# Three homes instead of two for a pair of experts' row indices, weights and flags

## The chip, the cores and the metric

The kernel runs on one core of a Trainium2 chip. The metric is the device time of one execution in microseconds (us); a kernel is represented by the median of its runs.

## The reference

Three layers follow each other: attention with a position bias, a dense MoE layer with the activation h·sigmoid(h), and a second MoE layer in which each token is routed to two of eight experts. The change lies in the last one:

```python
def _moe2_ref(x, w_gate, w_noise, noise, w1, w2):
    logits = x @ w_gate
    noise_scale = np.log1p(np.exp(x @ w_noise))
    noisy_logits = logits + noise_scale * noise
    top2 = np.argpartition(-noisy_logits, 2, axis=1)[:, :2]
    ...                                    # top2_w: softmax over the two
    for e in range(E):                     # E = 8, D = 512, F = 1024, 1152 tokens
        for k in range(2):
            mask = top2[:, k] == e
            h = np.maximum(x[mask] @ w1[e], 0.0)
            out[mask] += top2_w[mask, k, None] * (h @ w2[e])
```

## The kernel before, in words

Attention and the dense layer fill roughly the first 500 us. The last 240 us or so are the second MoE layer, and only they matter here.

The eight experts are taken as four pairs, g = 0 to 3; "pair 3" is experts 6 and 7. Each expert has 320 slots for its tokens. The loop at L1044 traces, for each pair g below 3, three things side by side: `experts(g)` (the products of this pair), `conv_pair(g + 1)` (the weights of the next pair) and `gather_pair(g + 1)` (the token rows of the next pair). A scheduler then fixes one order of instructions per engine, from its own model of times; at run time every engine and every queue goes through its list in that order, and an instruction that waits holds up all that stand behind it on the same engine.

For one pair the steps are:

- `gather_pair`: DVE makes 0/1 tables of slots (`one_hot`, L816); PE turns them into sums (`place`, L827, tile `pm`); DVE turns the sums into row numbers. That is `locate`: L840 writes `idx`, L842 `far` (a flag for an empty slot), L843 the second half of `idx`, and L849 and L850 write `ws`, the routing weights.
- `fetch`: POOL issues five gathers of token rows (L859, `gx<-yrows,idx`, 128 rows of 1024 fp16 values), and SP issues for each a transposing DMA into `xg` (L861). There are four `gx` buffers, so the fifth gather needs the first transpose done. A transpose waits for its gather.
- `conv_pair`: for each of the pair's four matrices, four loads of 512 KB on the SP queue (L909 for a first matrix, L911 for a second, tile `stg`, four buffers); ACT writes the high fp16 half (L923), DVE the low half (L924), which frees the `stg` buffer.
- `experts`: `up` is 16 blocks of 12 matmuls (L979 to L981) into one of three PSUM buffers `ph`. ACT writes the high half of the hidden rows (L985) and DVE the low half (L986); a `ph` buffer is free when both have read it. `down` (L995 to L997) and `down_last` (L1010) multiply by the second matrices into `po`; ACT scales a finished `po` by `ws` into `ot` (L964), and POOL adds it to the rows of `out` by an indirect DMA that reads the row numbers from `idx` (L958, "scatter" below). A pair has six scatters, and each waits for the one before it to land.

The homes of `idx`, `ws` and `far` for pair 0 are fixed (L884, L885, they show as `room`). Pairs 1, 2 and 3 call `slots_for`, which takes them from a pool with a number of buffers under one tag. With two buffers, pair 3 gets the ones that pair 1 had, so `locate` of pair 3 (L840) can write only when all that reads pair 1's is over; the last of that is pair 1's sixth scatter.

Of the kernel before, what the change touches and what calls it, by code (L numbers as in the profile page):

```python
# [9 lines left out]
F32 = mybir.dt.float32  # L10
F16 = mybir.dt.float16
I32 = mybir.dt.int32
# [4 lines left out]
DRAM = bass.MemoryType.DRAM  # L17
# [13 lines left out]
TOFF = 569  # L31
# artanh(s) / s = 1 + sum ARTANH[k] (4 s^2)^(k + 1) on 0 <= s <= 1/3, to float32
ARTANH = [0.0833333445274358, 0.012499649295167536, 0.0022356941233917663, 0.0004185089430942374, 0.00011865690887866284]
# [47 lines left out]
def shape_constants():  # L81
    """Tables that follow from the shapes alone."""
    f = np.float32
    pos = np.arange(S)
    lrel = np.log1p(pos.astype(f)).astype(f)
    psi = np.log1p(np.maximum(pos.astype(f), f(1.0))).astype(f)
    u = np.arange(TW)
    dist = np.abs(u[None, :] - TOFF - 2 * np.arange(4)[:, None])
    key = np.concatenate([256 * m + 2 * np.arange(n) + t for m, n in ((0, 128), (1, 128), (2, 32)) for t in range(2)])
    p = np.arange(128)  # L90
    row = np.zeros((128, NTT), f)
    for c in range(4):
        for b in range(B):
            row[:, 2 * c + b] = b * S + I0[c] + p
    row[:64, 8] = 512 + p[:64]
    row[64:, 8] = S + 512 + p[:64]
    return {
        "imax": np.ascontiguousarray(np.maximum(pos, 1).astype(f)[None, :] - f(0.5)),
        "ldist": np.log1p(dist.astype(f)).astype(f),
        "xij": (lrel[np.abs(pos[:, None] - key[None, :])] / psi[:, None]).astype(f),  # L100
        "bd": np.ascontiguousarray(np.repeat(np.eye(4, dtype=f), HID, axis=0)),
        "tri": (p[:, None] < p[None, :]).astype(np.float16),
        "eye": np.eye(128, dtype=np.float16),
        "iota": np.broadcast_to(np.arange(1, CAP + 1, dtype=np.float16), (128, CAP)).copy(),
        "row": np.ascontiguousarray(np.stack([1 + np.arange(NTT)[None, :] * 128 + p[:, None], row + 1], -1).astype(f)),
    }


def body(ctx, tc, nc, A):
    out = A["out"]  # L110
# [3 lines left out]
    def STT(eng, o, x, scale, y, op=OP.subtract):  # L114
        """o = x * scale - y"""
        if eng is G and scale == 1.0:
            G.tensor_tensor(o, x, y, op=op)  # L117
        else:
            V.scalar_tensor_tensor(o, x, scale, y, op0=OP.mult, op1=op)

    def after(later, earlier):
        """later issues behind earlier on their engine"""
        tc.add_manual_dep(later.ins, earlier.ins.name, mybir.DependencyInfo(
            mybir.DependencyClass.NoSync, mybir.DependencyReason.DATA), reason="order")
# [24 lines left out]

# [1 line left out]
    def load(name, shape, src, dt=F32, pool=main, eng=SP):  # L151
# [21 lines left out]
    def turn(dst, src, pe, ev):  # L173
        """dst[:, k] = the transpose of src's columns 128k .. 128k + 127."""
        if not pe:
# [10 lines left out]

    # the exponential's table is loaded while the data comes
    warm = at.tile([128, 1], F32, name="warm")
    G.memset(warm, 0.0)
    SC.activation(warm, warm, AF.Exp)  # L190
    # unit c at distance d is on where s*(max(i, 1) - 0.5) > s*tau, with s the sign of b1 and tau integral
    th4 = at.tile([128, 4], F32, name="th4")
# [29 lines left out]

# [1 line left out]
    KM = [at.tile([128, 2, H, 2, 128], F16, name=f"km{b}") for b in range(B)]  # L224
# [57 lines left out]
    def q_prep(c, g):  # L282
        """The first pass' columns of a head hold its high parts twice; the second's the low parts of both batches (or twice)."""
        nb = 2 if c < 4 else 1
# [24 lines left out]

# [1 line left out]
    EB = {c: dram.tile([H, NR[c], S], F32, name=f"eb{c}") for c in range(NCH) if c != ORDER[0]}  # L311

    BR = {}
    # eight places of 8 KB: the first chunk's position bias takes three, then weights in turn
    WB = main.tile([128, 8 * 4096], F16, name="wb")
# [62 lines left out]

# [1 line left out]
    def scores(c, h, qt, qs, pqs):  # L380
        """q k for the batches qs, or for both within a tile."""
        for _ in qs:
# [99 lines left out]

# [1 line left out]
    WT = {}  # L484

    def conv(key, half, src):
        """src(piece) -> DRAM view [128, 512] int64; 8 pieces of 512 columns."""
        hi, lo = wtile(), wtile()
# [35 lines left out]

# [1 line left out]
    wgn = m1.tile([128, 4, 16], F32, name="wgn", tag="th", bufs=NTH)  # L526
# [14 lines left out]
    def moe1(c):  # L541
        """h = x w_in, g = h sigmoid(h), f block by f block."""
        xT = xTs[c]
# [22 lines left out]
    def moe1b(c):  # L566
        """y = g w_out."""
        nb = 2 if c < 4 else 1
# [53 lines left out]
    def run(*gens):  # L622
        """gens: (generator, weight): round robin in proportion to the weights until all end."""
        live = [[g, w, 0.0] for g, w in gens if g is not None]
# [43 lines left out]
    a, b, c, d, e = ORDER  # L668
    # what is traced when: position of the first step, and distance of the steps
    live = {}  # L670

    def merge(until, **more):
        """steps of all that has been given, by position; each waits for the ends of those it names."""
        for name, (gen_, names) in more.items():
# [18 lines left out]
    for x in range(3):  # L693
        i = SP.dma_start(out[384 * x:384 * x + 384].rearrange("(t p) d -> p t d", p=128), zero[:, None, :].to_broadcast([128, 3, DM]))
        follow(i, ZK)
    # small tiles in what the position bias held
    homes = [("mk", 1024)] * 3 + [("btmp", 512)] * 3
# [28 lines left out]

# [1 line left out]
    T3 = [128, NTT, E]  # L728
# [13 lines left out]
    def route(t0, t1, part):  # L742
        """slot: 1 + the token's place among its expert's tokens, 0 for other experts; aux: 1 + its rows in Y and out, and its weight."""
        n = t1 - t0
        ts, T = slice(t0, t1), [128, n, E]
        lg, lx = LG[:, ts, :8], LG[:, ts, 8:]
        # log(1 + exp(x)) = max(x, 0) + 2 artanh(v / (2 + v)), v = exp(-|x|)
        V.scalar_tensor_tensor(u[:, ts], lx, -1.0, lx, op0=OP.mult, op1=OP.max)
# [30 lines left out]
        if part == 0:  # L779
            # later tokens take no slot below 128  # L780
            V.tensor_scalar(carry[:, 1], cnt, 128.0, None, op0=OP.max)
        else:
            V.tensor_tensor(carry[:, 0], carry[:, 1], cnt, op=OP.add)
# [18 lines left out]

# [1 line left out]
    # columns of 128 slots: 0 and 1 the first 128 of either expert, 2 and 3 the next 128, 4 both last 64, 5 the second's last 64 again  # L804
    XG, IDX, OHT, ROW = {}, {}, {}, {}
# [14 lines left out]
    def place(g, parts, f0, f1, pm):  # L820
        """sums over the tokens of aux's columns f0 .. f1, for each slot."""
        pm = pm[:, :6 * (f1 - f0)].rearrange("p (c f) -> p c f", c=6)
# [8 lines left out]
    def locate(g, *parts):  # L831
        """the rows of the slots of these columns, and unless that is urgent their weights; an empty slot reads row 0, and adds to a row past the end."""
        idx, ws = IDX[g]
# [18 lines left out]
    def fetch(g, part):  # L852
        """rows of Y for these slots, transposed."""
        idx = IDX[g][0]
# [8 lines left out]
    def slots_for(g):  # L863
        IDX[g] = (m2a.tile([128, 2, 6], I32, name="idx", tag="idx", bufs=2), m2a.tile([128, 5], F32, name="ws", tag="ws", bufs=2))
        ROW[g] = m2a.tile([128, 6], F32, name="far", tag="far", bufs=2)

    def dense(c):
        """the first MoE layer of one chunk, with the routing of the chunks before it."""
        for f, _ in enumerate(moe1(c)):
# [21 lines left out]

# [1 line left out]
    EW = {}  # L893

    def conv_half(e, half):
        """half 0: the expert's first matrix, 1: its second."""
        p = 4 * (e // 2) + 2 * half + e % 2
# [69 lines left out]
    def experts(g):  # L967
# [3 lines left out]
        def up(k, c0, n):  # L971
            """hidden rows for n columns of xg from c0; the second expert's begin at 320."""
            a_h, a_l = EW[2 * g + k, 0]
# [76 lines left out]
    s_m2.close()  # L1050
# [1 line left out]
    nround = nc.values_load(rounds[0:1, 1:2], min_val=0, max_val=13)  # L1052
# [81 lines left out]
```

## Time and profile before

| | us |
|---|---|
| median of 3 runs | 763.01 |
| the runs | 759.04, 763.01, 767.55 |
| span of the profiled execution (first to last instruction) | 761.8 |
| PE busy in it | 605.9 (80%) |
| DVE, ACT, POOL busy | 501.5, 378.1, 373.2 |
| granted TensorE clock, mean over the span | 0.894 of full speed |

The time of the profiled execution itself is not listed beside its span; the median lies 1.2 us above the span and the three runs lie 8.5 us apart. Times in the views count from the first instruction. A row of a timeline gives start, duration, engine, line, operation, tiles (written <- read), shapes, how many were merged, and in brackets the idle time of the engine before it and what ended it. "SPq" is the queue of DMAs that SP issues; the duration there is that of issuing, not of the transfer. Consecutive matmuls overlap in the records, so their pace is read from start to start.

### The profile page before, as it was taken

The numbers are of one execution on the slowest core, as the hardware profiler recorded it, in microseconds if no ns is written. First come the engines' busy times: TensorE is split into PE (matmuls) and PEld (weight loads), VectorE is DVE, ScalarE is ACT, GpSimd is POOL, SyncE is SP. The second block draws the span as 40 slices with busy tenths as digits, with TensorE's granted clock in tenths as the row PEclk, the third lists the DMA queues.
The fourth block names the chain that finished last, engine by engine and source line by source line (L and its number), as shares of the span: only waits on it lengthen the run. The fifth ranks groups of instructions, "written<-read, shape, count | busy, mean of one in ns | idle before, by whom it ended". The sixth has DMA issues, their size and how long they took to land. (4 is left out here: it accounts for less than half of the span.)

```text
span 761.8 us, 16564 instructions
## 1 busy us (share of the span) xinstructions
PE 605.9 (80%) x6371; PEld 401.7 (53%) x6371; DVE 501.5 (66%) x1093; ACT 378.1 (50%) x805; POOL 373.2 (49%) x366
## 2 busy tenths in 40 slices
PE   0564756568578888988998889969899899699992
PEld 0552434446344666556755665756665555355640
DVE  3999999999999689457943866546766625440200
ACT  2755558777544567355723654751464526241210
POOL 2786677678867687446842541305205122403022
PEclk9775557689698999998999999989999999899996
DMA  6457778779875699886996859635989847743123
GB/s 133 114 153 239 159 165 188 190 198 180 175 187 133 182 181 183 157 165 125 159 222 149 159 114 315 178 129 118 290 261 260 266 128 220 189 111 40 19 25 43
DMA packets 203143, 125.77 MB, mean 165 GB/s; under 512 B 153076, under 2 KB 175732, under 8 KB 203060
## 3 DMA queue, kind: packets, MB, share of 16 engines
q1 hardware_dynamic: 170868, 90.39, 51.2%
q10 hardware_dynamic: 27648, 24.32, 11.2%
q0 software_dynamic: 4544, 9.97, 7.0%
q8 instruction: 51, 0.84, 0.5%
q14 instruction: 32, 0.26, 0.1%
HBM read 74.83 MB, written 18.22 MB: 122 GB/s over the span
## 5 line engine op out<-in xcount | busy, mean ns | idle before, releaser
L117 POOL TENSOR_TENSOR pr<-z,pr 128x512 f16<-128x512 f32 x72 | 94.6, 1319 | 23.3 <-ACT pr L438 14.6
L553 PE MATMUL ph<-xT,wb 128*128 128x256 f16 (+1 forms) x320 | 84.3, 273 | 11.4 <-DVE th L558 5.9
L345 PE MATMUL pb<-rhs_h,mk 128*128 128x64 f16 (+1 forms) x720 | 66.4, 210 | 26.1 <-ACT ta L361 12.1
L337 DVE TENSOR_TENSOR mk<-io,tau 128x1024 f16<-128x1024 f16 (+1 forms) x90 | 85.2, 953 | 0.7 <-PE pb L346 0.7
L117 POOL TENSOR_TENSOR gt<-th,gt 128x256 f16<-128x256 f32 (+1 forms) x80 | 56.5, 709 | 59.3 <-ACT gt L562 56.7
L554 PE MATMUL ph<-xT,wb 128*128 128x256 f16 (+1 forms) x320 | 84.3, 273 | 0.0
L958 POOL DMA_INDIRECT out<-ot,idx x18 | 28.2, 1567 | 114.4 <-ACT ot L964 66.3
L117 POOL TENSOR_TENSOR g<-ta 128x256 f32<-128x256 f32 (+1 forms) x72 | 63.2, 877 | 42.9 <-ACT ta L361 36.0
L555 PE MATMUL ph<-xT,wb 128*128 128x256 f16 (+1 forms) x320 | 84.2, 273 | 0.0
L388 PE MATMUL pq<-km,qt 128*128 128x512 f16 (+2 forms) x160 | 51.5, 436 | 29.3 <-DVE st L431 28.8
L986 DVE SCALAR_TENSOR_TENSOR ht<-ph,ht 128x320 f16<-128x320 f32 (+2 forms) x80 | 32.7, 418 | 62.8 <-ACT ht L985 62.7
L436 ACT ACTIVATE z<-z,st 128x576 f32<-128x576 f32 x72 | 55.3, 768 | 37.2 <-DVE st L435 36.9
L345 PEld LDWEIGHTS <-mk 128*128 128x128 f16 (+1 forms) x720 | 57.9, 112 | 19.5 <-DVE mk L337 7.9
L346 PEld LDWEIGHTS <-mk 128*128 128x128 f16 (+1 forms) x720 | 57.0, 112 | 19.5 <-issue 18.8
L346 PE MATMUL pb<-rhs_l,mk 128*128 128x64 f16 (+1 forms) x720 | 66.0, 210 | 0.0
L924 DVE SCALAR_TENSOR_TENSOR wb<-stg,wb 128x1024 f16<-128x1024 f32 (+1 forms) x48 | 48.1, 1040 | 18.6 <-ACT wb L923 18.5
L985 ACT ACTIVATE ht<-ph 128x320 f16<-128x320 f32 (+2 forms) x80 | 29.5, 379 | 61.2 <-PE ph L981 60.0
L923 ACT ACTIVATE wb<-stg 128x1024 f16<-128x1024 f32 (+1 forms) x48 | 41.9, 908 | 33.5 <-DMA stg<-in_e 33.3
L577 PE MATMUL py<-wb,gt 128*128 128x512 f16 x144 | 56.1, 390 | 1.6 <-POOL wb L511 1.6
L576 PE MATMUL py<-wb,gt 128*128 128x512 f16 x144 | 56.0, 391 | 1.5 <-DVE st L431 1.3
L578 PE MATMUL py<-wb,gt 128*128 128x512 f16 x144 | 55.9, 388 | 0.0
L511 POOL TENSOR_TENSOR wb<-tt,wb 128x512 f16<-128x512 f32 x32 | 43.7, 1366 | 17.2 <-ACT wb L510 17.0
(198 smaller groups left out, 1800.8 us busy)
## 6 DMA issues: line engine op xcount, KB each, us to landing
stg<-in_e SPq DMA_DIRECT2D x64, 512.0 KB, 5.2
raw<-in_w_in ACTq DMA_DIRECT2D x16, 512.0 KB, 4.9
raw<-in_w_out ACTq DMA_DIRECT2D x16, 512.0 KB, 3.7
bt<-eb SPq DMA_DIRECT2D x24, 288.0 KB, 3.4
eb<-g SPq DMA_DIRECT2D x12, 512.0 KB, 3.5
yrows<-yh SPq DMA_DIRECT2D x9, 256.0 KB, 4.2
out<-zero SPq DMA_DIRECT2D x3, 768.0 KB, 5.8
bt<-eb SPq DMA_DIRECT2D x16, 144.0 KB, 2.9
```

The costliest lines, as they stand in the source:

```text
L117: G.tensor_tensor(o, x, y, op=op)
L337: i = V.tensor_tensor(mk[:, :, :n], io16[:, None, i0:i0 + n].to_broadcast([128, 8, n]), tv, op=OP.is_gt)
L345: mm(pb[:n, :, t, :], m, rhs_h, start=True, stop=False)
L346: mm(pb[:n, :, t, :], m, rhs_l, start=False, stop=True)
L388: i = mm(pq[p0:p0 + n, :512].rearrange("p (m s) -> p m s", m=2), lt, KM[b][r0:r0 + nr, :, h].rearrange("p m x s -> p m (x s)"), start=star ...
L436: SC.activation(z, z, AF.Exp, bias=st[:, 2:3], scale=0.125, accum_out=sums[:, bi, h % 4:h % 4 + 1])
L553: mm(ph, hh[:, cs], xh, start=(j == 3), stop=False)
L554: mm(ph, hh[:, cs], xl, start=False, stop=False)
L555: mm(ph, hl[:, cs], xh, start=False, stop=(j == 0))
L576: mm(pys[i], gh, oh[:, cs], start=(f == 0), stop=False)
L577: mm(pys[i], gh, ol[:, cs], start=False, stop=False)
L578: mm(pys[i], gl, oh[:, cs], start=False, stop=(f == 15))
```

## The change

The pool gets three buffers instead of two for the three tiles, so that pairs 1, 2 and 3 each have their own:

```diff
     def slots_for(g):
-        IDX[g] = (m2a.tile([128, 2, 6], I32, name="idx", tag="idx", bufs=2), m2a.tile([128, 5], F32, name="ws", tag="ws", bufs=2))
-        ROW[g] = m2a.tile([128, 6], F32, name="far", tag="far", bufs=2)
+        IDX[g] = (m2a.tile([128, 2, 6], I32, name="idx", tag="idx", bufs=3), m2a.tile([128, 5], F32, name="ws", tag="ws", bufs=3))
+        ROW[g] = m2a.tile([128, 6], F32, name="far", tag="far", bufs=3)
```

All else in the diff are comments and docstrings, which were taken out. Since the scheduler sees fewer dependencies, the order of the instructions changes too, on DVE, POOL and SP, all of it around `locate` and `fetch` of pair 3. (On PE one matmul of a `down` moves behind a block of `up`; on ACT the order stays.)

On DVE, at `locate` of pair 3, as a difference. `ew_9475` is the first matrix of expert 6, `ew_9661` that of expert 7, and L986 writes the hidden rows of pair 2:

```order
-L986 SCALAR_TENSOR_TENSOR ht<-ph,ht 128x320 x3
-L924 SCALAR_TENSOR_TENSOR ew_9475<-stg,ew_9474 128x1024 x4
-L924 SCALAR_TENSOR_TENSOR ew_9661<-stg,ew_9660 128x1024
...
+L986 SCALAR_TENSOR_TENSOR ht<-ph,ht 128x320 x2
 L840 TENSOR_SCALAR idx<-pm 128x5
 L842 TENSOR_SCALAR far<-pm 128x5
...
+L924 SCALAR_TENSOR_TENSOR ew_9475<-stg,ew_9474 128x1024 x4
+L924 SCALAR_TENSOR_TENSOR ew_9661<-stg,ew_9660 128x1024
```

`locate` moved ahead of the low halves of both first matrices of pair 3, eight instructions of L924, and ahead of four of L986. Before, L840 stood behind them and waited for the scatters of pair 1; now the only thing that it waits for is `pm` from PE.

On POOL, at the scatters of pair 1 (`idx_8318` is pair 1's, `idx_9500` pair 3's, `idx_8895` pair 2's), as a difference:

```order
 L958 DMA out<-ot_9307,idx_8318 1152x512
+L859 DMA gx_9763<-yrows_139,idx_9500 128x1024
+L859 DMA gx_9766<-yrows_139,idx_9500 128x1024
+L859 DMA gx_10056<-yrows_139,idx_9500 128x1024
+L859 DMA gx_10059<-yrows_139,idx_9500 128x1024
 L958 DMA out<-ot_9312,idx_8318 1152x512
+L859 DMA gx_10062<-yrows_139,idx_9500 128x1024
 L958 DMA out<-ot_9342,idx_8318 1152x512
```

The five gathers of pair 3 stood behind all six scatters of pair 1; now four stand behind the first scatter and the fifth behind the second.

On SP, the loads of pair 3's weights and the transposes of its rows, as a difference (the eight L909 are the loads of the first matrices of experts 6 and 7, four each):

```order
-L909 DMA stg<-in_e 128x1024 x8
-L911 DMA stg<-in_e 128x2x512 x5
-L861 DMA_TRANSPOSE xg<-gx 128x8x128 x2
-L911 DMA stg<-in_e 128x2x512 x3
-L861 DMA_TRANSPOSE xg<-gx 128x8x128 x3
+L909 DMA stg<-in_e 128x1024 x4
+L861 DMA_TRANSPOSE xg<-gx 128x8x128 x5
+L909 DMA stg<-in_e 128x1024 x4
+L911 DMA stg<-in_e 128x2x512 x8
```

All five transposes now stand between the loads for expert 6 and those for expert 7; before, thirteen loads stood ahead of the first of them.

## Rows read from the trace of the kernel before

**Rows 1.** The page, its first line.

```profile
span 761.8 us, 16564 instructions
```

**Rows 2.** The chain that ended last, 700 us on: start, us, what.

```profile
711.53 16.71 issue
```

**Rows 3.** Stretches: length, busy per engine (x instructions), PE clock, DMA share, GB/s.

```profile
530.00:553.00 23.00, 19.84 (x195) 14.29 (x192) 16.33 (x41) 7.84 (x14) 7.78 (x6) 1.00 1.03 283
618.00:632.00 14.00, 14.00 (x73) 6.92 (x71) 0.99 (x2) 2.71 (x4) 4.65 (x4) 1.00 0.26 31
640.00:653.70 13.70, 7.38 (x47) 4.55 (x47) 6.39 (x16) 8.92 (x13) 3.18 (x2) 0.91 0.79 222
653.70:658.00 4.30, 4.28 (x16) 2.19 (x16) 4.30 (x7) 0.44 (x1) 4.00 (x2) 0.51 0.61 169
658.00:728.00 70.00, 70.00 (x462) 40.05 (x461) 17.21 (x29) 18.21 (x34) 12.63 (x10) 1.00 0.37 75
```

**Rows 4.** Timeline of PE, 638 to 662 us.

```profile
639.95 0.38 PE L995 MATMUL po<-wb,ht 128*128 128x512 f16 x1 [0.32 <-ACT ot L964]
...
647.00 0.38 PE L996 MATMUL po<-wb,ht 128*128 128x512 f16 x1
653.72 0.42 PE L979 MATMUL ph<-xg,wb 128*128 128x320 f16 x1 [6.34 <-DVE ht L986]
...
661.72 0.62 PE L1010 MATMUL po<-wb,ht 128*64 128x512 f16 x4
```

**Rows 5.** Timeline of DVE, 640 to 660 us.

```profile
644.28 1.21 DVE L924 SCALAR_TENSOR_TENSOR ew<-stg,ew 128x1024 f16<-128x1024 f32 x1
652.51 0.17 DVE L840 TENSOR_SCALAR idx<-pm 128x5 int32<-128x5 f32 x1 [7.01 <-issue]
...
653.19 0.47 DVE L986 SCALAR_TENSOR_TENSOR ht<-ph,ht 128x320 f16<-128x320 f32 x1
```

**Rows 6.** Timeline of POOL, pair 1's first and last scatter, pair 3's gathers.

```profile
616.74 1.42 POOL L958 DMA_INDIRECT out<-ot,idx  x1 [18.96 <-ACT ot L964]
...
644.50 2.42 POOL L958 DMA_INDIRECT out<-ot,idx  x1 [6.94 <-ACT ht L985]
652.95 1.01 POOL L859 DMA_INDIRECT gx<-yrows,idx  x1 [6.02 <-DVE idx L843]
654.26 4.13 POOL L859 DMA_INDIRECT gx<-yrows,idx  x1 [0.30 <-issue]
658.70 1.19 POOL L859 DMA_INDIRECT gx<-yrows,idx  x1 [0.31 <-issue]
```

**Rows 7.** Timeline of PE, the sums for pair 3's `locate`.

```profile
615.63 1.59 PE L827 MATMUL pm<-room,oht 128*128 128x5 f16 x51
```

**Rows 8.** Timeline of the SP queue: loads for expert 7, last transpose of pair 3.

```profile
632.75 1.46 SPq L909 DMA_DIRECT2D stg<-in_e  x2
...
671.15 1.25 SPq L861 DMA_TRANSPOSE xg<-gx  x1
```

**Rows 9.** Waits of the SP queue, 612.6 to 640 us: total, times, longest.

```profile
SPq L909 <- DVE ew L924: 22.4, 4, 20.2
```

**Rows 10.** Timelines of POOL and SP, pair 1's first gather and last transpose.

```profile
530.84 1.00 POOL L859 DMA_INDIRECT gx<-yrows,idx  x1 [0.95 <-DVE far L842]
...
551.60 1.25 SPq L861 DMA_TRANSPOSE xg<-gx  x1
```

**Rows 11.** Timeline of ACT, 636 to 660 us: conversions of pair 3's weights.

```profile
638.27 1.06 ACT L923 ACTIVATE ew<-stg 128x1024 f16<-128x1024 f32 x1 [3.39 <-DMA stg<-in_e]
...
651.06 1.06 ACT L923 ACTIVATE wb<-stg 128x1024 f16<-128x1024 f32 x1 [0.23 <-DMA stg<-in_e]
657.11 0.44 ACT L985 ACTIVATE ht<-ph 128x320 f16<-128x320 f32 x1 [5.00 <-PE ph L981]
```

**Rows 12.** Line 909, 632 to 637 us: from issue to landing.

```profile
DMA to landing us min/median/max: 5.5/5.8/6.0
```

**Rows 13.** Line 909, 577 to 584 us, beside pair 2's gathers and transposes.

```profile
DMA to landing us min/median/max: 4.6/6.7/6.9
```

**Rows 14.** Line 861, transposes of pair 0 from 522 to 530 us.

```profile
DMA to landing us min/median/max: 3.1/3.1/3.1
```

**Rows 15.** Line 859, pair 3's gathers, 652 to 662 us.

```profile
DMA to landing us min/median/max: 3.3/4.2/6.9
```

## The prediction, made before the changed kernel was run

> **What bounds the kernel now.** I read the chain that ended last first. The end is a string of scatters, and ahead of it stands one wait of 16.71 us until 728.2 [rows 2], which is POOL waiting for PE's products of pair 3. So the end of the kernel moves with PE. Second, the table of stretches: from 618 to 632 PE is busy all 14.00 us, from 658 to 728 all 70.00 us, but from 640 to 653.7 only 7.38 of 13.70 [rows 3]. Third, PE's timeline shows that this is a single hole: the matmul at 647.00 ends at 647.38, the next starts at 653.72, 6.34 us later, released by L986 on DVE [rows 4]. Fourth, DVE: L924 from 644.28 ends at 645.49, then DVE stands still for 7.01 us until L840 of pair 3 starts at 652.51; the L986 that PE needs stands behind it and runs at 653.19 [rows 5]. The view names no instruction as releaser. What fits is pair 1's sixth scatter, issued at 644.50 [rows 6]: it reads the `idx` that L840 overwrites, and a landing at about 652.4 would be 7.9 us after issue. This is the wait that the change removes. After the hole PE also runs slowly: from 653.7 to 658 the granted clock is 0.51, that is 1.2 of 2.4 GHz, and full again from 658 on [rows 3].
>
> **The change, part by part.**
>
> *The hole.* L840 no longer waits for a scatter and stands before the four-plus-four L924 of pair 3's first matrices. Its only input is `pm`, whose 51 matmuls end at 617.22 [rows 7]; DVE has 0.99 us of work from 618 to 632 [rows 3], so `locate` (about 1 us) lies in idle time and costs nothing; if that cover were gone it would cost its 1 us. At 645.5 DVE goes straight on to L986, and PE's next block finds its `ph` buffer free by about 646. PE keeps its 6.34 us.
>
> *The clock.* The 4.30 us at clock 0.51 follow the hole; ahead of it PE was at full clock (from 640 to 653.7 the mean is 0.91, the fall lies inside the hole) [rows 3]. Without the hole the same work takes 4.30 x 0.51 = 2.2 us, a gain of 2.1. Sum so far 6.34 + 2.1 = 8.4 us.
>
> *Is something else late next on PE?* From 653.72 to the first L1010 at 661.72 PE needs 8.00 us [rows 4], 5.9 at full clock, so L1010 now comes at 647.2 + 5.9 = 653.1. It needs the high half of a hidden block that ACT writes behind its last conversion: that one starts at 651.06, just after its load landed, ends at 652.12, and with 0.44 for L985 the block is ready at 652.6 [rows 11]. So PE does not wait, but has only 0.5 us to spare.
>
> *Gathers, in POOL's queue.* The first follows scatter 1 (616.74 + 1.42) [rows 6] at about 618.5. Four gathers at about 1.3 us each push scatter 2 to 623.7, and the fifth gather follows at about 626.7, when the first transpose has landed. The later scatters of pair 1 move back by some 3 us, and the sixth may start at 648 instead of 644.5. Now only pair 2's first scatter waits for it, and that needs the `down_last` of pair 2, whose first matmuls run at 661.72 [rows 4].
>
> *Transposes, in SP's queue.* This is the price of the change. The four loads for expert 7 went out from 632.75 [rows 8], after the SP queue had stood idle for 20.2 us waiting for DVE to free their buffers [rows 9]. They now stand behind all five transposes. What arrives late hits PE at once: ACT's conversion at 638.27 had already waited 3.39 us for the first of these loads [rows 11], and PE at 639.95 had waited 0.32 us for the L964 behind it [rows 4]. So every us by which these loads land later is a us of PE. Two bounds. Upper: from the first gather to the end of the last transpose pair 3 took 652.95 to 672.40 = 19.4 us [rows 6, 8]. From 618.5 that ends at 637.9, 5.2 us after 632.75, and the load then lands 0.9 us slower (medians 6.7 beside gathers and transposes, 5.8 as it was) [rows 12, 13]: 6.1 us. Lower: gathers land 4.2 us after issue (median) [rows 15], so the first transpose goes out at 622.7 and lands at 626; the fifth gather lands at 630.9, its transpose takes 1.25 to issue and is through at 632.2, half a us before the loads could go anyway: 0. I take 0.5 us, near the lower end, because the stretch resembles that one: DMA share 0.26 from 618 to 632, against 0.61 to 0.79 and 1.03 where the long paces were measured [rows 3], and transposes in a quiet stretch landed after 3.1 us [rows 14]. A gain from this move is excluded: the loads still wait for DVE.
>
> Two rules of the Trainium skill bear on these 0.5 us. The rows first: a load took 0.9 us longer beside gathers and transposes. The page "DMA: Bandwidth & Descriptors", section "Issuing engines are not separate DMA queues", says that DMAs issued by SP and POOL run on the same 16 engines and interleave, which speaks against the change; by it a load that meets the last transpose would cost up to those 0.9 us even if SP issues it in time, and the trace agrees with it. Second, the gather at 654.26 took 4.13 us to issue, beside DVE's L924, and the one after it 1.19 [rows 6]. [...]
>
> **Sum.** 6.34 + 2.1 - 0.5 = 7.9 us. The span of 761.8 [rows 1] becomes 753.9; the median of the runs lies 1.2 above that span, so I predict **755.1 us**, 1.0% less than 763.01.
>
> **The rivals.**
>
> *The loads come late (in part given back).* Between 1 and 6.1 us late by the reckoning above. For it: both measured paces are near 20 us, and the queue is strictly in order. Against: both were measured with weight loads between the transposes and a DMA share above 0.6, where the new place has 0.26. Time: 763.0 - 8.4 + 1 to 763.0 - 8.4 + 6.1, so **755.6 to 760.7**.
>
> *ACT is the next to be late.* The spare 0.5 us at L1010 goes if the loads of expert 6's second matrix, for which ACT waited up to the end (0.23 at 651.06 [rows 11]), land later than before; the delayed scatters 5 and 6 now overlap them. A load 0.9 us slower would cost 0.4, one at 6.9 instead of 5.5 costs 0.9: **755.5 to 756**, too small to be told from the forecast.
>
> *Slower than before.* One mechanism: the fifth gather waits for the first transpose, the fifth transpose for that gather, and behind it on SP stand the loads. In pair 1 the way from the first gather to the end of the last transpose took 530.84 to 552.85 = 22.0 us, at a DMA share of 1.03 [rows 3, 10]. From 618.5 that is 640.5, the loads are 7.7 late and land 0.9 slower, PE stands for 8.6 us from 640 on, falls to half clock as it did after 6.34 us, and pays the 2.1 again: 10.7 lost for 8.4 won, **765.3**. It decides from 6.3 us of lateness on, where lateness and clock together eat the 8.4. For it speaks only that stretch, and it carried nine times the DMA traffic (283 against 31 GB/s, to which the moved gathers and transposes add).
>
> *The change does nothing.* This would need another reader of the old home, or another wait of L840. The order shows three separate homes and `pm` as the only wait: **763**.
>
> **How the numbers follow.** Forecast 0.65, loads late 0.20, ACT late 0.08, slower 0.05, nothing 0.02. The runs of before spread over 8.5 us, so a median of three may be off by some 2.5 us; 1% (7.6 us) is about what can be told from no change. The range runs from 755.1 less 2.5 and a little for a lateness of 0, to the top of the late loads: **752 to 761**. Faster by over 1% means under 755.4: a bit over half of the forecast's 0.65, a third of ACT's 0.08 and little of the others, 0.41. Slower by over 1% means over 770.6, which even the slower rival reaches only with the spread or a longer pace: 0.04. The rest, 0.55, is within 1%, most of it a real gain of some us.
>
> **What would show it.** Right: on DVE L840 of pair 3 starts near 617.5 with no idle time of 7 us before it; PE's hole of 6.34 us is gone, the clock is 1.00 from 640 to 658, and the first L1010 behind it comes at about 653; on SP the fifth transpose is through by 633; ACT's wait for the load that was 3.39 us stays under 4.5. Wrong: the loads for expert 7 go out after 634, or PE stands at 640 for more than 1 us, or a new hole opens between 640 and 665. If the hole is gone and PE gains nothing by 728, the premise that the end moves with PE is wrong.

## The result and the profile after

The changed kernel takes **758.37 us** (median of 17 runs, 749.10 to 766.24), beside 764.80 us for the kernel before timed beside it (17 runs, 759.04 to 770.23). The ratio is **0.9889, 95% interval 0.9863 to 0.9915**; it leaves out four runs of the changed kernel that count as slow, more than 1.5% above its fastest (760.48 to 766.24 us), and the medians of all 17 runs each give 0.9916. The forecast was 755.1 of 763.01, a ratio of 0.9896; the absolute time lies 3.3 us above it and inside the range, partly because the kernel before was itself 1.8 us higher when both were timed together.

The page of the changed kernel opens with:

```profile
span 756.6 us, 16562 instructions
```

That is 5.2 us less than [rows 1], but this execution entered the second MoE layer late: pair 1's first scatter starts at 620.14, against 616.74 in [rows 6], although nothing was changed ahead of it (over the twelve profiled executions of this document it starts between 613.85 and 622.00). So times of after are compared less 3.4 us, and the stage is measured from that scatter to pair 3's first: 616.74 to 728.47 before, 620.14 to 723.38 after, 111.7 and **103.2 us, 8.5 less**. Behind pair 3's first scatter both executions need 33.3 and 33.2 us. Pair 3's first scatter on POOL's timeline, in the kernel before:

```profile
728.47 1.42 POOL L958 DMA_INDIRECT out<-ot,idx  x1 [20.28 <-ACT ot L964]
```

And in the changed kernel:

```profile
723.38 1.43 POOL L958 DMA_INDIRECT out<-ot,idx  x1 [20.26 <-ACT ot L964]
```

Stretches of the changed kernel, with the columns of [rows 3]:

```profile
618.00:632.00 14.00, 14.00 (x120) 7.91 (x119) 1.84 (x9) 3.56 (x6) 7.77 (x7) 1.00 0.78 188
640.00:653.70 13.70, 13.33 (x90) 8.59 (x89) 9.47 (x12) 9.48 (x14) 2.54 (x2) 1.00 1.02 323
653.70:658.00 4.30, 4.30 (x27) 2.09 (x25) 3.05 (x5) 1.71 (x3) 1.57 (x1) 1.00 1.02 360
658.00:723.00 65.00, 65.00 (x433) 37.52 (x431) 15.56 (x27) 17.87 (x33) 9.11 (x6) 1.00 0.20 33
```

PE is busy 13.33 of the 13.70 us in which it had been busy 7.38, and the clock is 1.00 throughout. On DVE's timeline L840 stands early, and L986 follows the fourth conversion of expert 7 without a pause:

```profile
621.51 0.17 DVE L840 TENSOR_SCALAR idx<-pm 128x5 int32<-128x5 f32 x1 [1.74 <-PE pm L827]
...
647.74 1.22 DVE L924 SCALAR_TENSOR_TENSOR ew<-stg,ew 128x1024 f16<-128x1024 f32 x1
648.87 1.12 DVE L986 SCALAR_TENSOR_TENSOR ht<-ph,ht 128x320 f16<-128x320 f32 x2
```

L840 now waits for its sums alone (compare [rows 5]). PE's only gap over 0.25 us between 605 and 700 us is the one that was there before [rows 4], and the first L1010 of pair 2 comes at 653.2 on the old time axis:

```profile
643.41 0.38 PE L995 MATMUL po<-wb,ht 128*128 128x512 f16 x1 [0.37 <-ACT ot L964]
...
656.62 0.62 PE L1010 MATMUL po<-wb,ht 128*64 128x512 f16 x4
```

POOL's timeline: the first scatter of pair 1, the first two gathers of pair 3, and the fifth:

```profile
620.14 1.42 POOL L958 DMA_INDIRECT out<-ot,idx  x1 [19.34 <-DMA stg<-in_e]
621.95 1.02 POOL L859 DMA_INDIRECT gx<-yrows,idx  x1 [0.38 <-DVE idx L843]
623.26 0.98 POOL L859 DMA_INDIRECT gx<-yrows,idx  x1 [0.30 <-issue]
...
630.05 0.98 POOL L859 DMA_INDIRECT gx<-yrows,idx  x1 [1.51 <-DMA xg<-gx]
```

The SP queue: five transposes, then the four loads for expert 7, which stood in front of them before [rows 8]:

```profile
625.32 11.62 SPq L861 DMA_TRANSPOSE xg<-gx  x5
637.03 2.85 SPq L909 DMA_DIRECT2D stg<-in_e  x4
```

The loads go out 16.9 us after pair 1's first scatter, 0.9 later than before (632.75 - 616.74 = 16.0). ACT's conversion nonetheless waits hardly longer, 3.44 us against the 3.39 of [rows 11]:

```profile
641.72 1.06 ACT L923 ACTIVATE ew<-stg 128x1024 f16<-128x1024 f32 x1 [3.44 <-DMA stg<-in_e]
```

And the chain that ended last now runs through the landing of that load, 4.58 us after its issue (in the kernel before the view follows the chain back only to 701 us, so the two can't be compared here):

```profile
637.03 4.58 DMA stg<-in_e
```

### The profile page after: what moved, and what is told of

It reads as the page before. It is cut to its first block, busy times and chain, and to the rows that moved or that the text cites. A ratio compares the mean times of both kernels' runs of the same rounds, so it can differ in the third digit from the quotient of the medians.

```text
span 756.6 us, 16562 instructions
## 1 busy us (share of the span) xinstructions
PE 606.9 (80%) x6371; PEld 402.6 (53%) x6371; DVE 502.3 (66%) x1093; ACT 377.9 (50%) x805; POOL 366.5 (48%) x366
## 4 chain that ended last, share of the span: by engine, by line
PE 29%; DVE 29%; DMA 18%; issue 11%; ACT 4%; POOL 4%; SPq 3%; ACTq 1%; another core or an unknown queue 1%; DVEq 0%; POOLq 0%
DMA stg<-in_e 6%; DVE mk L337 4%; PE ph L979 3%; DVE z L431 3%; DMA pt<-pr 3%; PE ph L981 3%; DVE pr L442 3%; PE ph L980 3%; DVE tt L504 3%; DVE tt L505 3%; PE po L1010 3%; DVE tt L500 2%; PE po L996 2%; PE po L995 2%; PE po L997 2%
## 5 line engine op out<-in xcount | busy, mean ns | idle before, releaser
L553 PE MATMUL ph<-xT,wb 128*128 128x256 f16 (+1 forms) x320 | 84.9, 275 | 11.5 <-DVE th L558 7.1
L986 DVE SCALAR_TENSOR_TENSOR ht<-ph,ht 128x320 f16<-128x320 f32 (+2 forms) x80 | 32.8, 420 | 54.3 <-ACT ht L985 53.8
L924 DVE SCALAR_TENSOR_TENSOR wb<-stg,wb 128x1024 f16<-128x1024 f32 (+1 forms) x48 | 48.3, 1042 | 23.6 <-ACT wb L923 20.2
```

The source lines that it names most:

```text
L553: mm(ph, hh[:, cs], xh, start=(j == 3), stop=False)
```

## The experiments

**The theory.** The third home of `idx` takes away L840's wait for pair 1's last scatter; that wait cost PE a hole and half clock behind it. The price is paid on SP: what pushes back the loads for expert 7 is lost on PE. **Rivals:** another of the three homes counts; the loads have slack; the rows must be early for the gain.

All edits are made to the changed kernel. The table has one profiled execution each: when the first load for expert 7 is issued (after pair 1's first scatter), PE's gaps over 0.3 us behind that scatter, what ran at 1.2 GHz behind a gap, the time from pair 1's first scatter to pair 3's, and the ratio to the kernel before with its interval.

| kernel | load at | PE's gaps | at 1.2 GHz | scatter to scatter | ratio |
|---|---|---|---|---|---|
| before | 16.0 | 0.32, 6.34 | 4.30 | 111.7 | 1 |
| the change | 16.9 | 0.37 | none | 103.2 | 0.9889 [0.9863, 0.9915] |
| the change again | 17.6 | 0.93 | none | 103.9 | 0.9934 [0.9899, 0.9968] |
| two rings of landing buffers | 17.9 | 0.88 | none | 103.8 | 0.9921 [0.9881, 0.9962] |
| `idx` alone | 18.0 | 1.14, 0.89 | none | 105.0 | 0.9927 [0.9896, 0.9958] |
| `ws`, `far` alone | 16.0 | 0.48, 5.15 | 4.32 | 111.0 | 1.0012 [0.9978, 1.0046] |
| three homes, late | 15.6 | 1.08 | none | 104.7 | 0.9966 [0.9936, 0.9996] |
| two homes, late | 15.6 | 0.49, 0.81, 0.44 | none | 105.7 | 0.9932 [0.9897, 0.9967] |
| two landing buffers | 25.9 | 9.44 | 4.81 | 114.8 | 1.0034 [0.9999, 1.0069] |
| transposes among loads | 16.0 | 1.16, 0.41, 1.79 | none | 106.3 | 0.9941 [0.9905, 0.9976] |
| transposes behind all loads | 16.0 | none | none | 102.8 | 0.9923 [0.9896, 0.9950] |

The gaps and half of the stretch at half clock account for the fifth column: for the kernel before 0.32 + 6.34 + 2.1 - 0.37 = 8.4 over the change (8.5 measured), for two landing buffers 9.44 + 2.4 - 0.37 = 11.5 (11.5). Only the two late kernels, whose order on PE differs, need 0.8 and 1.1 us more than their gaps explain; part of it is that all 51 matmuls of L827, the sums for pair 3's `locate`, lie inside their stretch (busy 2.25 us, in the change 0.48), and the rest stays open. In the others the sum comes within 0.4.

### Three homes for the row indices alone

```diff
-... name="ws", tag="ws", bufs=3), ... name="far", tag="far", bufs=3)
+... name="ws", tag="ws", bufs=2), ... name="far", tag="far", bufs=2)
```

> Three homes for the row indices (idx) alone; weights (ws) and flags (far) keep two. Theory A, the wait removed was for the home of idx, which pair 1's last scatters still read: the time is that of the change, 0.989 of before (0.985 to 0.993); L840 of pair 3 starts within 2 us of the end of L827's 51 matmuls, PE has no gap over 0.5 us from the first L964 of pair 1 to the end of pair 3, and the granted clock is 1.00 for the 40 us behind it. L849 and L850, which write ws, stand some 26 us further back on DVE; nothing of pair 3 wants them before its first L964, so they cost nothing. Theory B, ws or far was the home that was held: L840 or L842 waits as before, the hole of 6.3 us with some 4 us of half clock behind it stays, 1.00 (0.996 to 1.004). Theory C, each of the three homes gives a part: something between, 0.992 to 0.996, with a hole of 2 to 4 us.

Measured: 0.9927 (0.9896 to 0.9958). DVE's timeline of this kernel, at `locate` of pair 3:

```profile
618.30 0.16 DVE L840 TENSOR_SCALAR idx<-pm 128x5 int32<-128x5 f32 x1 [0.89 <-PE pm L827]
```

Its SP queue, the transposes and the loads for expert 7:

```profile
622.96 12.73 SPq L861 DMA_TRANSPOSE xg<-gx  x5
635.79 1.96 SPq L909 DMA_DIRECT2D stg<-in_e  x4
```

And its PE, both gaps over 0.3 us:

```profile
641.82 0.38 PE L995 MATMUL po<-wb,ht 128*128 128x512 f16 x1 [1.14 <-ACT ot L964]
...
655.99 0.62 PE L1010 MATMUL po<-wb,ht 128*64 128x512 f16 x4 [0.89 <-ACT ht L985]
```

The hole and the half clock are gone, so `idx` alone does it. (The time by itself would fit theory C as well; the trace decides.) "No gap over 0.5 us" was missed: here the transposes took 12.73 us of SP's queue in place of 11.62, the loads went out 18.0 us after the scatter, and PE paid at both places that the prediction had named as its next limits, L995 and L1010.

### Three homes for weights and flags alone

```diff
-... name="idx", tag="idx", bufs=3)
+... name="idx", tag="idx", bufs=2)
```

> The reverse: three homes for weights and flags, two for the row indices. The instructions stand on POOL, SP, DVE and ACT as in the kernel before. Theory A (idx alone counts): 1.00 of before (0.996 to 1.004); DVE stands still for 6 to 8 us ahead of L840 of pair 3, PE's hole of 6.3 us with half clock behind it is back. Theory B (ws or far): 0.989. Theory C (each a part): 0.992 to 0.996.

Measured: 1.0012 (0.9978 to 1.0046), as theory A said. DVE's timeline, where the wait stands:

```profile
650.67 0.17 DVE L840 TENSOR_SCALAR idx<-pm 128x5 int32<-128x5 f32 x1 [5.83 <-DMA out<-ot,idx]
...
651.35 0.47 DVE L986 SCALAR_TENSOR_TENSOR ht<-ph,ht 128x320 f16<-128x320 f32 x1
```

POOL's timeline, the sixth scatter of pair 1:

```profile
643.41 1.55 POOL L958 DMA_INDIRECT out<-ot,idx  x1 [6.67 <-issue]
```

PE's timeline at the end of the hole:

```profile
651.88 0.42 PE L979 MATMUL ph<-xg,wb 128*128 128x320 f16 x1 [5.15 <-DVE ht L986]
```

The stretch behind it, with the columns of [rows 3]:

```profile
651.88:656.20 4.32, 4.32 (x16) 2.21 (x16) 4.32 (x7) 1.08 (x2) 4.01 (x2) 0.50 0.58 180
```

DVE's row settles what the prediction had to infer: in [rows 5] the releaser of L840 is only "issue", here the same wait carries its name, a scatter into `out`. That sixth scatter lands 7.1 us after its issue, and L840 starts 0.2 us later; the wait of 5.83 us is a little under the 6 to 8 expected. The trace of the kernel before records the landing of its sixth scatter too, issued at 644.50 and so landed at 652.3, just ahead of L840 at 652.51 (7.9 us was assumed). Line 958, 644.4 to 646 us:

```profile
DMA to landing us min/median/max: 7.8/7.8/7.8
```

And the hole is again followed by 4.3 us at 1.2 GHz.

### The rows of pair 3 later, with three homes and with two

```diff
-(gather_pair(g + 1), 2))
+(chain([None] * 1 if g == 2 else [], gather_pair(g + 1)), 2))
```

The edit puts one empty step ahead of pair 3's `gather_pair`, so that it is issued later. In the second kernel `bufs=2` is put back for all three as well.

> Three homes, but pair 3's locate, gathers and transposes are issued one step later, so L840 stands behind the conversions L924 of expert 6 and 7 on DVE, the gathers behind all six scatters of pair 1 on POOL and the transposes behind all 16 loads on SP. Theory A, the gain is made of two things, no wait ahead of L986 and the rows of pair 3 ready when PE wants them: the hole near 645 is gone and the clock stays 1.00 there, but L840 runs some 37 us later than in the change (near 654 on the time axis of the kernel before), the last transpose is through 15 to 19.4 us after it and lands 3 us later, 671 to 675.5, where PE wants the rows near 669: PE stands for 2 to 7 us there, and up to 2 us more are lost if the clock falls. That is 2 to 9 us over the change, 0.991 to 1.001 of before. Theory B, only the wait ahead of L986 counted and the rows have slack wherever they are gathered: 0.989, no gap over 1 us.

> The same later place for pair 3's locate, gathers and transposes, with two homes for all three as before. L840 now has to wait for pair 1's scatters again. Theory A, the wait costs PE only because L986 stands behind it on DVE: at the later place the sixth scatter (issued near 644.5, landed near 652.4) is through before or within 1 us of L840's turn near 654, so the time is that of the three homes at the same late place within 0.3%, the hole near 645 is gone, and a gap opens at the rows of pair 3: 0.991 to 1.001 of before. Theory B, whatever is written into a home that a scatter holds costs the 6 us wherever it stands: 2 us or more over the three homes at the same place, and a DVE wait of 5 us or more ahead of L840.

Measured: 0.9966 (0.9936 to 0.9996) and 0.9932 (0.9897 to 0.9967); the intervals overlap. With three homes, DVE's timeline at L840:

```profile
654.22 0.15 DVE L840 TENSOR_SCALAR idx<-pm 128x5 int32<-128x5 f32 x1
```

The transposes of pair 3 on its SP queue:

```profile
660.02 9.60 SPq L861 DMA_TRANSPOSE xg<-gx  x5
```

And PE's first product of pair 3:

```profile
672.77 0.30 PE L979 MATMUL ph<-xg,ew 128*128 128x320 f16 x1
```

With two homes, DVE's timeline at L840:

```profile
651.16 0.15 DVE L840 TENSOR_SCALAR idx<-pm 128x5 int32<-128x5 f32 x1
```

And PE's first product of pair 3:

```profile
668.81 0.30 PE L979 MATMUL ph<-xg,ew 128*128 128x320 f16 x1 [0.44 <-DMA xg<-gx]
```

With two homes L840 finds its old home free (the sixth scatter, issued at 641.73, landed 6.8 us later, 2.6 us ahead of L840) and waits for nothing, and the hole is gone without a third home: the wait had cost PE only because L986 stood behind it. That half of theory A held. The other half failed: the expected stall of 2 to 7 us at pair 3's first L979 is 0 and 0.44 us. The last transpose is issued by 50.8 us after pair 1's first scatter (669.62 - 618.81), and PE comes to the rows at 54.0, in the change at 52.0. What PE has more of ahead of them is the 51 matmuls of L827 (18 in the change), five of L1010 (48 against 43) and a longer gap (1.08 us against 0.37); L995 to L997 are as many as in the change. Theory B's 0.989 was not reached either by the trace (1.5 and 2.5 us over the change).

### Two landing buffers for the gathers, and the control

```diff
-gx = m2a.tile([128, 2 * DM], F16, name="gx", tag="gx", bufs=4)
+gx = m2a.tile([128, 2 * DM], F16, name="gx", tag="gxb" if c % 2 and g < 3 else "gxa", bufs=2)
```

The control leaves out `and g < 3`, so pair 3 has four buffers again.

> The change, with the five gathers of pair 3 on two landing buffers (gx) in place of four. On POOL they then stand as two gathers, two scatters, two gathers, a scatter, a gather, and each later pair waits for earlier transposes. The order on SP, DVE, ACT and PE is that of the change. This takes the price that the prediction put at 0.5 us and makes it large. Theory A, every us by which the transposes push back the loads for expert 7 is a us of PE: the loads, issued 16.9 us after pair 1's first scatter in the change, go out at about 22 to 27 us after it (the first two gathers land 5 us after issue, the next two stand behind the second and third scatter, the fifth behind the fourth), 5 to 10 us later; PE stands 5 to 10 us ahead of the L995 that waits for ot, behind ACT's conversion waiting for its load, and from 6 us on falls to 1.2 GHz behind it, which costs up to 2 us more. 5 to 12 us over the change, 0.996 to 1.005 of before. Theory B, the loads have slack that the trace doesn't show (they land faster once the gathers are done): under 2 us over the change, 0.989 to 0.992.

> Control for the run with two landing buffers: the landing buffers of all gathers in two rings of two in place of one ring of four, so four as in the change, and the instructions stand on every engine as in the change. All theories: the time of the change, 0.989 of before (0.986 to 0.993). It is also a second look at the price of the moved transposes: from pair 1's first scatter to the first load for expert 7 16.0 us in the kernel before, 16.9 in the change, 18.0 with three homes for the indices alone; PE's gap ahead of the first L995 was 0.32, 0.37 and 1.14. If lateness goes to PE with a slack of about 1 us, a gap here is (first load minus 17) within 0.5 us.

Measured: 1.0034 (0.9999 to 1.0069) with two, 0.9921 (0.9881 to 0.9962) in the control. With two buffers, the SP queue:

```profile
622.49 20.69 SPq L861 DMA_TRANSPOSE xg<-gx  x5
643.28 1.96 SPq L909 DMA_DIRECT2D stg<-in_e  x4
```

ACT's timeline, the first conversion of expert 7 that waits:

```profile
648.00 1.06 ACT L923 ACTIVATE ew<-stg 128x1024 f16<-128x1024 f32 x1 [12.51 <-DMA stg<-in_e]
```

PE's timeline:

```profile
649.69 0.58 PE L995 MATMUL po<-wb,ht 128*128 128x512 f16 x1 [9.44 <-ACT ot L964]
```

The stretches of the hole and behind it:

```profile
640.25:649.69 9.44, 0.00 (x1) 0.02 (x2) 0.60 (x1) 1.69 (x3) 1.17 (x1) 0.73 0.95 269
649.69:654.50 4.81, 4.81 (x14) 1.98 (x14) 4.59 (x7) 3.76 (x6) 1.84 (x1) 0.50 0.76 211
```

The control, the loads for expert 7 on the SP queue:

```profile
631.71 1.96 SPq L909 DMA_DIRECT2D stg<-in_e  x4
```

And PE's only gap:

```profile
637.62 0.38 PE L995 MATMUL po<-wb,ht 128*128 128x512 f16 x1 [0.88 <-ACT ot L964]
```

Theory A: the loads go out 25.9 us after the scatter, 8.1 later than in the control, and PE's gap is 8.6 longer. Up to about 17 us there is slack (gaps of 0.32 at 16.0 and 0.37 at 16.9), from there lateness goes to PE one for one; the control, 0.9 us above 17, has its forecast gap (0.88). This is the prediction's slower rival made real: third home kept, gain eaten, 3.1 us more than before from scatter to scatter.

### The transposes behind the loads

(`after(later, earlier)` fixes the order of two instructions on one queue.) First, pair 3's transposes ordered behind the four loads for expert 7's first matrix; then behind all 16 loads (the fifth gather follows the scatters in both).

```diff
-LAST["xg", part] = SP.dma_start_transpose(...)
+LAST["xg", part] = SP.dma_start_transpose(...); g == 3 and after(LAST["xg", part], LAST["ld", 7, 0])
```

> The change, with the five transposes of pair 3 ordered behind the four loads for expert 7's first matrix on SP; on POOL the fifth gather then stands behind all six scatters of pair 1, and the transposes lie among the loads for the second matrices. Theory A, the transposes ahead of the loads cost 0 to 2 us of PE from one execution to the next: the loads go out 16.0 us after pair 1's first scatter as in the kernel before, the gap ahead of L995 is 0.3 to 0.5 us, the rows of pair 3 are still in time (the last transpose some 45 us after that scatter, wanted by PE at 52), and the time is that of the change less 0 to 2 us, 0.986 to 0.989 of before. Theory B, the transposes now hurt the loads for the second matrices, behind which ACT stands with 0.5 us to spare: a gap of 1 to 4 us ahead of L1010 or L979 between 35 and 55 us after that scatter, 0.990 to 0.994.

Measured: 0.9941 (0.9905 to 0.9976), theory B. PE's timeline, its gaps:

```profile
652.79 0.30 PE L979 MATMUL ph<-xg,wb 128*128 128x320 f16 x1 [1.16 <-DVE ht L986]
654.99 0.30 PE L979 MATMUL ph<-xg,wb 128*128 128x320 f16 x1 [0.41 <-DVE ht L986]
659.12 0.30 PE L979 MATMUL ph<-xg,wb 128*128 128x320 f16 x1 [1.79 <-DVE ht L986]
```

The loads of second matrices (L911, from 640 to 662 us): who waited for them, how long, how often, and the landing of the one load for which it is recorded:

```profile
  ACT wb L923: 9.5, 6
...
DMA to landing us min/median/max: 7.5/7.5/7.5
```

The gap at L995 is gone, but ACT now waits 9.5 us, in six waits, for loads that lie between transposes (1.5 us, in one, in the change). Moving the price does not remove it.

```diff
-for c in range(2, 5) if part else range(2):
+for c in cs or (range(2, 4 if g == 3 else 5) if part else range(2)):
...
+held.append(lambda c=c, gx=gx: SP.dma_start_transpose(...)); g == 3 and not cs or LAST.update({("xg", part): held.pop()()})
...
+run(...); g == 2 and ([after(t(), LAST["ld", 7, 1]) for t in fetch.__defaults__[1]], ..., fetch(3, 1, [4]))
```

> The change, with pair 3's five transposes behind all 16 weight loads on SP; four of its gathers stay where the change has them, the fifth stands behind the six scatters of pair 1. PE, DVE and ACT keep the order of the change. Theory A, only what stands ahead of a load on SP costs PE anything, and the rows have 10 us or more to spare: the loads for expert 7 go out 16.0 us after pair 1's first scatter as in the kernel before, the gap ahead of L995 is 0.3 to 0.5 us, no gap over 0.5 us follows it (where the transposes between the loads for the second matrices left three of 3.4 us in all), the last transpose is through near 46 us after that scatter and PE wants the rows at 52. From pair 1's first scatter to pair 3's first 103.0 to 103.5 us; by the time 0 to 1 us below the change, which the runs can hardly tell: 0.986 to 0.990 of before. Theory B, the rows come late: a gap ahead of pair 3's first L979 of 1 to 6 us, 104 to 109 us from scatter to scatter, 0.990 to 0.997.

> The change itself, beside the run with the transposes behind all loads, on the same chip. 0.989 of before (0.986 to 0.993). A third execution of this order to see what the moved transposes cost: loads for expert 7 issued 16.9 (change) and 17.9 us (two rings of landing buffers) after pair 1's first scatter went with gaps of 0.37 and 0.88 ahead of L995, and 103.2 and 103.8 us from scatter to scatter; this one should lie between 16.0 and 18.5, 0.3 and 1.5, 103.0 and 105.

> The same kernel as the one with pair 3's transposes behind all 16 loads, timed again because the first interval (0.9758 to 0.9937) rests on two runs. By its trace (102.8 us from pair 1's first scatter to pair 3's first, 103.2 to 103.9 in three executions of the change's order, 111.7 in the kernel before) it is 0.4 to 1.1 us below the change: 0.985 to 0.991 of before. If the trace of the one execution was a lucky one: above 0.993, with gaps over 0.5 us ahead of L995 or L979.

The first timing gave 0.9847 (0.9758 to 0.9937), an interval that rests on two of six runs, since one at 747.03 lay far below the other five (757.96 to 759.16); the second 0.9923 (0.9896 to 0.9950). One lies below and one above the 0.986 to 0.990 expected, and the second also above its own 0.985 to 0.991. The change itself, run beside the first: 0.9934 (0.9899 to 0.9968), just above its 0.993. Of the second timing's execution, the SP queue:

```profile
634.29 3.73 SPq L909 DMA_DIRECT2D stg<-in_e  x4
...
655.29 11.96 SPq L861 DMA_TRANSPOSE xg<-gx  x5
```

The landing of these loads, which have no transpose near them (line 909, 634 to 639 us):

```profile
DMA to landing us min/median/max: 5.4/6.2/7.0
```

And PE's first product of pair 3, without a gap:

```profile
669.88 0.30 PE L979 MATMUL ph<-xg,ew 128*128 128x320 f16 x1
```

Of the change run again, the loads on the SP queue:

```profile
634.34 2.11 SPq L909 DMA_DIRECT2D stg<-in_e  x4
```

And PE's gap behind them:

```profile
640.53 0.38 PE L995 MATMUL po<-wb,ht 128*128 128x512 f16 x1 [0.93 <-ACT ot L964]
```

Theory A by the trace: no gap, rows in time, 102.8 us from scatter to scatter in both executions, 0.4 to 1.1 under the change's order. By the time no difference can be shown.

## Why the prediction was right

*The hole of 6.34 us* went as predicted: L840 at 618.1 on the old axis (617.5 forecast), L986 straight behind L924. The home of `idx` was the cause, shown by the two kernels that split the three homes.

*The clock, 2.1 us,* was right too: 1.00 from 640 to 658, the first L1010 at 653.2 where 653.1 was forecast. The two experiments with a hole show the same price behind it, 4.32 and 4.81 us at 0.50.

*The 0.5 us for late loads* came out right in size by luck, since two errors cancelled. The transposes were through at 633.5 on the old axis (632.2 to 633 forecast): the fifth gather was issued at 626.65 as reckoned (626.7), but landed 5.5 us later instead of 4.2. So the loads were issued 0.9 us late, and 1.6 to 2.0 in three more executions with the same order on SP, more than the forecast had. Against that they landed no slower, as the prediction had feared, but sooner: the first one after 4.58 us in the change, and in 5.0 and 5.2 us with `idx` alone and in the control (medians of two recorded loads each), against the 5.8 of [rows 12]. Why they landed sooner is not shown. Over these four executions the gap at L995 grew by 0.05, 0.61, 0.56 and 0.82 us, 0.5 on average. The first rule weighed, from the Trainium skill's "DMA: Bandwidth & Descriptors", section "Issuing engines are not separate DMA queues", is that DMAs of several engines interleave on the same DMA engines; from it the prediction took up to 0.9 us for a load that meets the last transpose. The loads went out right behind it, at 637.03 in the change, where it had been issued at 635.59 and the shortest landing in [rows 14] is 3.1 us, so they most likely met it, and no such price shows. A load that lay between transposes, in the experiment above, took 7.5 us, which fits the rule; but a load with no transpose near took 7.0 in the run with the transposes behind all loads, so the transposes are not shown to be what slowed it.

*ACT with 0.5 us to spare* was a fair reading: no gap at L1010 in the change, 0.89 in the execution with `idx` alone.

*The upper bound of the lateness and the slower rival* were sound as a mechanism. It did not happen, since four landing buffers let the gathers run ahead; with two, the loads were 9.9 us later than before (7.7 reckoned), PE stood for 9.44 us (8.6) and lost 2.4 to the clock (2.1), and the stage took 3.1 us more than before (2.3).

*The sum.* 7.9 us forecast; 8.5 by the trace of the change and 6.8 to 8.0 in the three other executions with the same order of scatters and loads. By the time, the change gives 1.1% (0.8% by the medians of all runs) and its repetition 0.7%. Intervals of 0.3% either way are about 2 us, so whether the median gains a us less than the stage does is left open.

## What to carry to other kernels

A tile that an indirect DMA reads is held until that DMA lands, here 7 to 8 us after the issue of a pair's last scatter; look at what stands behind the next writer on its engine, because that is what pays. A further buffer and a later place for the writer both take the wait away; which is better is decided by what else moves with it. On an in-order queue, count everything that the moved step puts ahead of a load: here about 1 us was free, and from there each us was lost.

## What was not expected of the hardware

A load that lies between transposes took 7.5 us to land, those behind them 4.2 to 5.7 (the `idx` experiment, where the loads for expert 7 follow all five) and those with no transpose near 5.4 to 7.0 (the transposes behind all loads). Gathers beside an idle DVE took 0.94 to 1.02 us to issue, and 4.13 beside L924 in the kernel before [rows 6] and again with `ws` and `far` alone; but in the two late kernels the fifth gather, issued beside a row of four L924, took only 1.78 and 1.52 us. POOL's timeline with three homes, late:

```profile
664.36 1.78 POOL L859 DMA_INDIRECT gx<-yrows,idx  x1 [4.91 <-DMA xg<-gx]
```

And DVE's beside it:

```profile
662.96 4.63 DVE L924 SCALAR_TENSOR_TENSOR wb<-stg,wb 128x1024 f16<-128x1024 f32 x4 [1.06 <-ACT wb L923]
```

The Trainium skill's "SBUF — State Buffer", section "SBUF: two separate sides", says that a DVE operation with two SBUF inputs contends with POOL over the ports that they share only where the POOL operation reads SBUF. A gather reads `idx`, but that this is what slowed these gathers no run here shows. Gaps of PE up to 1.79 us left the clock at full speed; those of 5.15 us and more were followed by 4.3 to 4.8 us at 1.2 GHz.
